# Rounding of the feed-forward weights in three VectorE operations, its range guard as a later check of refetched pieces, and the first half batch's softmax sums on TensorE

## The chip, the cores and the metric

The kernel runs on one core of one Trainium2 chip. The metric is the device time of one execution in microseconds (us). The engines are named as in the profile: PE is TensorE (PEld its weight load), DVE is VectorE, ACT is ScalarE, POOL is GpSimd and SP is SyncE, which here only issues transfers. Each engine works through its own instructions in order.

## What is computed

An attention block with routing by cluster is followed by a feed-forward block. Queries and keys attend to each other only where both have the same nearest centroid.

```python
q_assign = argmax(einsum('bhsd,hcd->bhsc', q_n, c_n), axis=-1)   # batch 4, heads 8, seq 768, dim 64
k_assign = argmax(einsum('bhsd,hcd->bhsc', k_n, c_n), axis=-1)   # 16 clusters
mask = q_assign[:, :, :, None] == k_assign[:, :, None, :]
attn = softmax(where(mask, scale * q @ k.T, -1e9))
x = (attn @ v).transpose(0, 2, 1, 3).reshape(3072, 512)
h = x @ w_in                                                     # w_in 512 x 2048
out = (h - tanh(h)) @ w_out                                      # w_out 2048 x 512
```

The two weight matrices arrive as 64-bit floats, that is as pairs of 32-bit words, and the kernel makes 32-bit floats of them on the chip.

## The kernel before

**Steps.** The work runs through 96 steps. A *block* is half of a batch's queries (8 blocks). In it four *pairs* of heads follow each other, and each pair takes three steps, of two key tiles of 128 each. In a step `begin` (L476) makes the scores of the following step: `score` (L319) multiplies on PE into a tile `sc` of the PSUM pool `ps_s`, which has two buffers, and ACT takes the exponential in place. `select` (L330) then has DVE mask them by equal cluster codes, four operations a step, into `e`; POOL adds the masked tiles up into `sum` (L346, L350). `value` (L353) multiplies `e` by `v` on PE. After a pair's third step `total` (L367) has PE sum `sum` over the partitions into `den`, ACT copies it to SBUF, POOL adds it into `wholes` (L380), and `divide` (L383) takes reciprocals on DVE, whose result POOL adds into `inverses` (L390). Both are read at the very end by a range check that decides whether a general version (`general`, L571) has to run.

**Feed-forward.** From the second block on, 28 items of `ffn_items` (L394) of the half batch before are spread over a block's 12 steps: 16 `up` items (PE multiplies by `w_in`, ACT takes tanh, DVE subtracts: `h`, `th`, `g`) and 12 `project` items (PE multiplies by `w_out` into `o`). `h`, `o` and `den` share the PSUM pool `ps_f` of three buffers. Small work (`todo`, L534) is handed out between the items of a step.

**Routing a pair.** Each later pair of heads is prepared by four stages that `ready` (L446) assigns to steps: 0 is `turn` (PE transposes of q and k into `pt`, also in `ps_s`, and two ACT copies), 1 is `similar` (PE product with the centroids into `sim`, ACT copy `simt`), 2 is `route` (PE transposes of `simt`, four DVE operations that give `code`), 3 is `publish` (a PE transpose of `code`, a DVE cast, a store to DRAM, from which `spread` loads `row` again). `sim`, the transposes of `simt` and that of `code` all lie in one buffer of `ps_s`, held from stage 1 to stage 3. Stages 1 and 2 stand at the end of one step, and stage 3 at the very start of the next, ahead of `begin`.

**Weights.** 32 pieces of 512 KB each go through three buffers `raw`, fetched by POOL's queue (L131). `round_weights` (L135) has ACT scale the low words into `rest`, DVE shift and mask the high words (L146, L150), and POOL add the two as integers (L153). `guard_weights` (L155), one piece later, has DVE take the exponent out of the high words again (L162) and multiply the result by whether it is in range (L166); only then is the `raw` buffer free and the next piece fetched. `weights_on` (L466) does one piece in each of the first block's 12 steps (two before them) and three in each step of the second block until all 32 are done, in its first six steps.

Of the kernel before, what the change touches and what calls it, by code (L numbers as in the profile page):

```python
# [28 lines left out]
F32 = mybir.dt.float32  # L29
# [7 lines left out]
P = 128  # L37
BIG = 2.0**60
F32_LEAST = 897
TINY = 1e-30  # L40
# [9 lines left out]
def kernel(  # L50
# [29 lines left out]

    const = ctx.enter_context(tc.tile_pool(name="const", bufs=1))
# [8 lines left out]
    wholes = const.tile([P, TB], F32, name="wholes")  # L90
    flag = const.tile([1, 1], I32, name="flag")
# [11 lines left out]
    ] + [(w_out[c // FQ][:, c % FQ], w_out_r[:, c]) for c in range(CF)]  # L103

    def fast():
# [27 lines left out]
        rests = {}  # L133

        def round_weights(n: int):  # L135

            if words == 1:
                return  # L140
            bits = PIECES[n][0].bitcast(U32)
            pair = raws[n].rearrange("p (n two) -> p n two", two=2)
            lo, hi = pair[:, :, 0], pair[:, :, 1]
            rest = rests[n] = outp.tile([P, FQ * P], U32, name="rest", tag="osb")
            nc.scalar.activation(out=rest, in_=lo, func=ACT.Copy, scale=2.0**-29)
            nc.vector.tensor_scalar(  # L146
                out=bits, in0=hi, scalar1=3, scalar2=0x3FFFFFF8,
                op0=ALU.logical_shift_left, op1=ALU.bitwise_and,
            )
            nc.vector.scalar_tensor_tensor(  # L150
                out=bits, in0=hi, scalar=0xC0000000, in1=bits, op0=ALU.bitwise_and, op1=ALU.bitwise_or
            )
            nc.gpsimd.tensor_tensor(out=rest, in0=bits, in1=rest, op=ALU.add)  # L153

        def guard_weights(n: int):  # L155

            if words == 1:
                return
            dst = PIECES[n][0]
            bits = dst.bitcast(U32)  # L160
            hi = raws.pop(n).rearrange("p (n two) -> p n two", two=2)[:, :, 1]
            nc.vector.tensor_scalar(  # L162
                out=bits, in0=hi, scalar1=20, scalar2=0x7FF,
                op0=ALU.logical_shift_right, op1=ALU.bitwise_and,
            )
            nc.vector.scalar_tensor_tensor(  # L166
                out=dst, in0=bits, scalar=float(F32_LEAST), in1=rests.pop(n).bitcast(F32),
                op0=ALU.is_ge, op1=ALU.mult,
            )
# [86 lines left out]
        def similar(n: int):  # L256

            ps = sims[n] = ps_s.tile([P, 2, 512], F32, name="sim", tag="s")
            for i in range(2):
                for half in range(2):  # L260
                    r = (2 * i + half) * 2 * C
                    nc.tensor.matmul(  # L262
                        ps[r : r + 2 * C, 0, 0:TB], lhsT=bd[:, pairs[n][1]],
                        rhs=turned[n, i][:, half], start=True, stop=True, tile_position=(0, r),
                    )
            t = rtp.tile([P, TB], F32, name="simt")
            nc.scalar.copy(out=t, in_=ps[:, 0, 0:TB])
            sims[n] = ps, t

        def route(n: int):  # L270

            ps, t = sims.pop(n)
            for j in range(HCH):
                nc.tensor.transpose(  # L274
                    out=ps[:, 1, j * P : (j + 1) * P], in_=t[:, j * P : (j + 1) * P], identity=ident
                )
            G = HCH * 8
            pr = ps[:, 1, 0:TB].rearrange("p (g c) -> p g c", c=C)
# [14 lines left out]
            sims[n] = ps, code  # L293

        def publish(n: int):
            ps, code = sims.pop(n)
            G = HCH * 4
            nc.tensor.transpose(  # L298
                out=ps[0:G, 0, 0:P], in_=code[:, 0].rearrange("p a h j -> p (a h j)"), identity=ident
            )  # L300
            t = rtp.tile([G, P], BF16, name="qc")
            nc.vector.tensor_copy(out=t, in_=ps[0:G, 0, 0:P])
# [27 lines left out]
        def select(n: int, half: int, j: int):  # L330
# [11 lines left out]
            if j % 2 == 1:  # L342
# [9 lines left out]
        def value(n: int, half: int, s: int):  # L352
# [11 lines left out]
        dens = {}  # L364

        def total(n: int, half: int):

# [366 lines left out]
```

## Time and profile before

| what | value |
|---|---|
| median of three runs (lowest, highest) | 1224.85 us (1223.64, 1228.05) |
| the profiled execution | 1225.34 us |
| its span, first to last instruction | 1223.6 us |
| PE busy | 1085.9 us (89%) |
| DVE busy | 550.4 us (45%) |
| POOL busy | 437.3 us (36%) |
| ACT busy | 307.3 us (25%) |

The span is what the trace shows from the first to the last instruction; 1.7 us of the profiled execution lie around it. Busy times are sums over stretches with different limits, so the table alone doesn't tell what ends last anywhere. A line of the trace's timeline has the start in us from the span's start, the duration in us (of all merged instructions), engine, source line, operation, output and inputs, the number of instructions, and in brackets the idle time of the engine before it with what ended it. A 32-bit matmul stands as two instructions in the trace.

### The profile page before, as it was taken

What the parts mean: (1) busy time and instruction counts of PE and PEld (TensorE: products, weight loads), DVE (VectorE), ACT (ScalarE), POOL (GpSimd) and SP (SyncE); (2) the same over time, 40 slices, a digit from 0 to 9 for tenths busy, and PEclk for the clock granted to TensorE, in tenths of its full rate; (3) what the DMA queues carried; (4) which work ended last, traced back from release to release, by engine and by line L of the source; (5) the groups of instructions that cost most, each with busy time, mean ns of one, the idle gap of its engine ahead of it and who ended that gap; (6) DMA issues with size and microseconds to landing.
All of it is one profiled execution on the core that took longest, in us unless ns stands there. A gap on an engine that the chain in (4) does not pass through costs nothing.

```text
span 1223.6 us, 10558 instructions
## 1 busy us (share of the span) xinstructions
PE 1085.9 (89%) x3842; PEld 506.0 (41%) x3842; DVE 550.4 (45%) x891; ACT 307.3 (25%) x491; POOL 437.3 (36%) x318
## 2 busy tenths in 40 slices
PE   3655676789889999889889999898889999999997
PEld 1222333334444445444345445443345445544543
DVE  3788998863344324333334333433334432442210
ACT  2332222222223122322123213222123223321100
POOL 1555665443223333233214432332324433443000
PEclk9777888899999999999889999999999999999999
DMA  7332234221020000112020000110000000000000
GB/s 194 104 84 71 67 118 118 83 58 54 22 52 7 9 18 13 43 44 54 22 52 7 9 9 22 33 46 32 33 20 7 16 16 9 1 9 9 9 9 21
DMA packets 66509, 49.10 MB, mean 40 GB/s; under 512 B 52624, under 2 KB 60816, under 8 KB 66448
## 3 DMA queue, kind: packets, MB, share of 16 engines
q1 hardware_dynamic: 59776, 25.22, 8.3%
q0 software_dynamic: 6528, 23.07, 5.6%
q8 instruction: 33, 0.54, 0.2%
q14 instruction: 28, 0.23, 0.1%
q10 hardware_dynamic: 144, 0.03, 0.0%
HBM read 41.98 MB, written 6.34 MB: 39 GB/s over the span
## 4 chain that ended last, share of the span: by engine, by line
PE 74%; DVE 12%; issue 9%; ACT 2%; DMA 2%; POOL 1%; SPq 0%; POOLq 0%; DVEq 0%; ACTq 0%
PE o L415 24%; PE h L402 22%; PE sc L323 13%; PE av L359 11%; DVE e L337 2%; PE den L372 2%; PE pt L244 1%; DVE w_in L150 1%; PE sim L262 1%; DVE w_in L166 1%; DVE w_out L150 1%; DMA raw<-in_moe_w_out_dram 1%; DVE den L386 1%; DVE w_in L146 1%; DVE top L287 1%
## 5 line engine op out<-in xcount | busy, mean ns | idle before, releaser
L402 PE MATMUL h<-xT,w_in 128*128 128x384 f32 x1024 | 348.4, 497 | 8.5 <-DVE g L409 8.5
L415 PE MATMUL o<-w_out,g 128*128 128x512 f32 x768 | 341.0, 598 | 0.0
L350 POOL TENSOR_TENSOR sum<-sum,e 128x768 f32<-128x768 f32 x128 | 232.1, 1813 | 275.5 <-DVE e L337 272.2
L337 DVE SCALAR_TENSOR_TENSOR e<-row,code,sc 128x384 f32<-128x384 bf16 x384 | 213.3, 608 | 258.5 <-ACT sc L328 198.8
L402 PEld LDWEIGHTS h<-xT,w_in 128*128 128x128 f32 x1024 | 193.6, 193 | 162.4 <-issue 30.2
L415 PEld LDWEIGHTS o<-w_out,g 128*128 128x128 f32 x768 | 142.4, 190 | 188.6 <-issue 184.7
L328 ACT ACTIVATE sc<-sc 128x768 f32<-128x768 f32 x192 | 146.2, 794 | 243.0 <-PE sc L323 213.7
L323 PE MATMUL sc<-t,t 64*128 64x384 f32 x768 | 180.6, 595 | 26.0 <-DVE e L337 14.4
L409 DVE TENSOR_TENSOR g<-h,th 128x384 f32<-128x384 f32 x128 | 71.1, 555 | 230.5 <-ACT th L407 230.0
L359 PE MATMUL av<-e,vals 128*64 128x384 f32 x768 | 156.3, 531 | 0.0
L407 ACT ACTIVATE th<-h 128x384 f32<-128x384 f32 x128 | 62.8, 491 | 295.3 <-PE h L402 293.1
L323 PEld LDWEIGHTS sc<-t,t 64*128 64x128 f32 x768 | 75.4, 214 | 110.2 <-issue 52.6
L380 POOL TENSOR_TENSOR wholes<-wholes,den 128x384 f32<-128x384 f32 x32 | 31.8, 993 | 198.0 <-ACT den L379 198.0
L386 DVE RECIPROCAL den<-den 128x128 f32<-128x128 f32 x96 | 83.2, 916 | 35.7 <-POOL wholes L380 35.7
L359 PEld LDWEIGHTS av<-e,vals 128*64 128x64 f32 x768 | 49.9, 146 | 103.4 <-issue 101.8
L423 POOL DMA_DIRECT2D out_dram<-osb x24 | 13.4, 558 | 165.0 <-ACT osb L422 165.0
L346 POOL TENSOR_TENSOR sum<-e 128x768 f32<-128x768 f32 x32 | 57.8, 1806 | 23.3 <-DVE e L337 22.4
L390 POOL TENSOR_TENSOR inverses<-inverses,den 128x384 f32<-128x384 f32 x32 | 43.8, 1370 | 46.4 <-DVE den L386 46.4
L298 PE MATMUL sim<-ident,code 128*12 128x128 f32 x16 | 5.4, 340 | 53.1 <-DVE code L289 53.1
L422 ACT COPY osb<-o 128x512 f32<-128x512 f32 x24 | 14.1, 589 | 145.7 <-PE o L415 145.7
L244 PE MATMUL pt<-ident,x 128*128 128x128 f32 x192 | 29.0, 306 | 22.7 <-DMA x<-in_q_dram 8.4
L282 DVE TENSOR_REDUCE mx<-sim 128x24 f32<-128x384 f32 x16 | 8.9, 555 | 73.9 <-PE sim L274 73.9
(66 smaller groups left out, 434.9 us busy)
## 6 DMA issues: line engine op xcount, KB each, us to landing
raw<-in_moe_w_in_dram POOLq DMA_DIRECT2D x16, 512.0 KB, 4.1
raw<-in_moe_w_out_dram POOLq DMA_DIRECT2D x16, 512.0 KB, 3.8
x<-in_q_dram SPq DMA_DIRECT2D x32, 192.0 KB, 3.8
x<-in_k_dram SPq DMA_DIRECT2D x32, 192.0 KB, 4.6
vals<-in_v_dram SPq DMA_DIRECT2D x32, 192.0 KB, 2.5
row<-q_codes SPq DMA_DIRECT2D x32, 192.0 KB, 3.2
out_dram<-osb POOLq DMA_DIRECT2D x24, 256.0 KB, 2.3
q_codes<-qc SPq DMA_DIRECT2D x16, 3.0 KB
```

Of the source, the lines that this page charges most:

```text
L323: nc.tensor.matmul(sc[:, h, 0:TB], lhsT=turned[n, 1][r].rearrange("p a n -> p (a n)")[:, j * P : (j + 1) * P], rhs=turned[n, 0][r, half], ...
L328: nc.scalar.activation(out=sc[:, :, 0:TB], in_=sc[:, :, 0:TB], func=ACT.Exp, scale=SCALE)
L337: nc.vector.scalar_tensor_tensor(out=e[:, h], in0=rows[n, half][:, h], scalar=codes[n][:, 1, j // HCH, h, j % HCH : j % HCH + 1], in1=sc[: ...
L346: nc.gpsimd.tensor_tensor(out=s, in0=pair[:, 0], in1=pair[:, 1], op=ALU.add)
L350: nc.gpsimd.tensor_tensor(out=s, in0=s, in1=pair[:, i], op=ALU.add)
L359: nc.tensor.matmul(avs[n, half][h * D : h * D + D], lhsT=vals[n][:, h, j], rhs=e[:, i, h], start=(j == 0), stop=(j == NCH - 1),)
L386: nc.vector.reciprocal(out=t[:, c], in_=t[:, c])
L390: nc.gpsimd.tensor_tensor(out=inverses, in0=inverses, in1=dens.pop((n, half)), op=ALU.add)
L402: nc.tensor.matmul(h, lhsT=w_in[i][:, c, o * P : (o + 1) * P], rhs=xT[b, half][:, c], start=(c == 0), stop=(c == CD - 1),)
L407: nc.scalar.activation(out=th, in_=h, func=ACT.Tanh)
L409: nc.vector.tensor_tensor(out=gs[i][:, o], in0=h, in1=th, op=ALU.subtract)
L415: nc.tensor.matmul(acc[sub], lhsT=gs[i][:, o, sub * P : (sub + 1) * P], rhs=w_out[i][:, o], start=(i == 0 and o == 0), stop=(i == NQ4 - 1 ...
```

## The change

- `assemble` replaces both `round_weights` and `guard_weights`: ACT scales the low words into `rest` as before, DVE shifts and masks (two operations), and DVE adds `rest` instead of POOL. The guard's two DVE operations per piece and POOL's add go away. The piece's `raw` buffer is free right after, and the next fetch follows at once.
- `check_weights`: when all 32 pieces are rounded, every piece is fetched again, one a step, and one DVE operation takes the smallest magnitude of its high words into a column of `smallest`. That joins the range check at the end (two small DVE operations more). `general` rounds and guards the pieces itself, in a branch that these inputs don't take.
- In the first block (`early`) the sums of `e` are made on PE: four matmuls a step with `ones` accumulate in `den`, in a buffer of `ps_f` that a pair holds for its three steps. POOL's sums and the summing matmuls of `total` go away there.
- `sim`, the transposes of `simt` (`pr`) and of `code` (`pq`) get buffers of `ps_f` of their own, each freed after its read, instead of one of `ps_s`.
- Stage 1 moves to the start of the next step, ahead of `begin`; stage 0 comes right after `select`; stages 2 and 3 come last in their steps, 3 one step after 2. Before the first step, `select` comes ahead of the second pair's preparation.

```diff
+    def assemble(dst, raw, rest):
+        nc.scalar.activation(out=rest, in_=lo, func=ACT.Copy, scale=2.0**-29)
+        nc.vector.tensor_scalar(
+            out=bits, in0=hi, scalar1=3, scalar2=0x3FFFFFF8,
+            op0=ALU.logical_shift_left, op1=ALU.bitwise_and,
+        )
+        nc.vector.scalar_tensor_tensor(
+            out=bits, in0=hi, scalar=0xC0000000, in1=bits, op0=ALU.bitwise_and, op1=ALU.bitwise_or
+        )
+        nc.vector.tensor_tensor(out=bits, in0=bits, in1=rest, op=ALU.add)
...
+        def check_weights(n: int):
             hi = raws.pop(n).rearrange("p (n two) -> p n two", two=2)[:, :, 1]
+            nc.vector.tensor_reduce(
+                out=smallest[:, n : n + 1], in_=hi.bitcast(F32), axis=AX.X, op=ALU.min,
+                apply_absolute_value=True,
             )
...
-            ps = sims[n] = ps_s.tile([P, 2, 512], F32, name="sim", tag="s")
+            ps = ps_f.tile([P, TB], F32, name="sim", tag="f")
...
+            ps = ps_f.tile([P, TB], F32, name="pr", tag="f")
...
+            ps = ps_f.tile([G, P], F32, name="pq", tag="f")
...
+            if early(n, half):
+                if s == 0:
+                    sums[n, half] = ps_f.tile([P, TB], F32, name="den", tag="f")
+                for i in range(2):
+                    for h in range(2):
+                        nc.tensor.matmul(
+                            sums[n, half][h * D : h * D + D], lhsT=ones, rhs=e[:, i, h],
+                            start=(s + i == 0), stop=(2 * s + i == NCH - 1),
+                        )
...
         def weights_on():
+            nonlocal done
+            if done < len(PIECES):
+                round_weights(done)
+            elif done < 2 * len(PIECES) and words == 2:
+                check_weights(done - len(PIECES))
+            done += 1
+            fetch()
...
-            if 3 in stages:
-                stages.pop(3)()
+            if 1 in stages:
+                stages[1]()
...
+            if 0 in stages:
+                todo.append(stages[0])
             todo += late
...
-            todo += [stages[i] for i in sorted(stages)]
+            todo += [weights_on] * (3 if block == 1 and done < len(PIECES) else 1)
+            todo += [stages[i] for i in (2, 3) if i in stages]
```

What this does to the order of instructions is shown at two places. The first is DVE in the first block, from a pair's third piece of weights to the division of its sums; `e` is the masked tile, `den` the sums. Before:

```order
L146 TENSOR_SCALAR w_in_69<-raw 128x512
L150 SCALAR_TENSOR_TENSOR w_in_69<-raw,w_in_69 128x512
L162 TENSOR_SCALAR w_in_69<-raw 128x512
L166 SCALAR_TENSOR_TENSOR w_in_69<-w_in_69,rest 128x512
L337 SCALAR_TENSOR_TENSOR e<-row,code,sc 128x384 x4
L386 RECIPROCAL den<-den 128x128 x3
L389 TENSOR_TENSOR xT<-xT,den 128x384
```

And with the change, the same place on DVE:

```order
L118 TENSOR_SCALAR w_in_69<-raw 128x512
L122 SCALAR_TENSOR_TENSOR w_in_69<-raw,w_in_69 128x512
L125 ISA w_in_69<-w_in_69,rest 128x1024
L335 SCALAR_TENSOR_TENSOR e<-row,code,sc 128x384 x4
L399 RECIPROCAL den<-den 128x128 x3
L402 TENSOR_TENSOR xT<-xT,den 128x384
```

The guard's two operations have gone, and the integer add has come from POOL; it is built as one special instruction on 1024 halves of words instead of 512 words.

The second place is PE where a later pair is routed, at the end of a block's projections; `simt` and `code` are what the transposes read, `sim` and `pr` what they write. Before:

```order
L415 MATMUL o<-w_out_73,g 128x512 x4
L262 MATMUL sim<-t_2662,bd 32x384 x2
L262 MATMUL sim<-t_2671,bd 32x384 x2
L274 MATMUL sim<-ident,simt 128x128 x3
L298 MATMUL sim<-ident,code 12x128
L323 MATMUL sc<-t_2349,t_2358 128x384 x4
L359 MATMUL av<-e,vals 64x384 x4
L372 MATMUL den<-sum,ones 64x384 x2
L415 MATMUL o<-w_out_74,g 128x512 x4
L415 MATMUL o<-w_out_75,g 128x512 x4
```

And with the change, the same pair on PE:

```order
L243 MATMUL pt<-ident,x_2401 128x128 x6
L261 MATMUL sim<-t_2722,bd 32x384 x2
L261 MATMUL sim<-t_2731,bd 32x384 x2
L321 MATMUL sc<-t_1663,t_1672 128x384 x4
L357 MATMUL av<-e,vals 64x384 x4
L428 MATMUL o<-w_out_73,g 128x512 x4
L428 MATMUL o<-w_out_74,g 128x512 x4
L274 MATMUL pr<-ident,simt 128x128 x3
L321 MATMUL sc<-t_2387,t_2396 128x384 x4
L357 MATMUL av<-e,vals 64x384 x4
L385 MATMUL den<-sum,ones 64x384 x2
L428 MATMUL o<-w_out_75,g 128x512 x4
```

`sim`, the transposes of `simt` and that of `code` stood back to back on PE, ahead of the next scores. Now scores, values and projections stand between `sim` and `pr`, the transpose of `code` (`pq`) comes two rows behind the last one shown, and `sim` follows right on the transposes `pt` of its stage 0.

## Rows read from the trace of the kernel before

**Rows 1.** Stretches: length; busy us (count) by engine; PE's clock, DMA share, GB/s.

```profile
42.00:141.00 99.00, 59.63 (x248) 24.73 (x248) 90.86 (x110) 31.95 (x48) 61.60 (x47) 0.74 0.28 79
141.00:254.00 113.00, 85.96 (x292) 41.49 (x288) 101.04 (x138) 34.11 (x58) 61.18 (x54) 0.86 0.32 100
327.00:1124.00 797.00, 767.10 (x2764) 357.56 (x2764) 298.85 (x516) 202.49 (x326) 278.15 (x182) 0.98 0.08 23
```

**Rows 2.** DVE's groups, 42 to 141 us: busy us, mean ns | idle before, releaser.

```profile
L337 DVE SCALAR_TENSOR_TENSOR e<-row,code,sc 128x384 f32<-128x384 bf16 x44 | 24.2, 604 | 7.0 <-ACT sc L328 6.6
L150 DVE SCALAR_TENSOR_TENSOR w_in<-raw,w_in 128x512 uint32<-128x512 uint32 x11 | 19.5, 1774 | 0.4
L166 DVE SCALAR_TENSOR_TENSOR w_in<-w_in,rest 128x512 f32<-128x512 uint32 x11 | 18.0, 1634 | 0.4
L146 DVE TENSOR_SCALAR w_in<-raw 128x512 uint32<-128x512 uint32 x11 | 13.2, 1198 | 0.0
L386 DVE RECIPROCAL den<-den 128x128 f32<-128x128 f32 x9 | 7.7, 912 | 1.2 <-POOL wholes L380 1.2
L162 DVE TENSOR_SCALAR w_in<-raw 128x512 uint32<-128x512 uint32 x11 | 4.6, 416 | 0.0
```

**Rows 3.** Timeline of one step of the first block, from 42 us.

```profile
42.35 2.83 PE L359 MATMUL av<-e,vals 128*64 128x384 f32 x8
43.36 3.77 POOL L350 TENSOR_TENSOR sum<-sum,e 128x768 f32<-128x768 f32 x2 [3.02 <-DVE e L337]
45.50 2.18 DVE L150 SCALAR_TENSOR_TENSOR w_in<-raw,w_in 128x512 uint32<-128x512 uint32 x1
...
48.05 1.63 DVE L166 SCALAR_TENSOR_TENSOR w_in<-w_in,rest 128x512 f32<-128x512 uint32 x1
```

**Rows 4.** DVE's timeline: each pair's first select, and one L150 between.

```profile
57.12 2.18 DVE L337 SCALAR_TENSOR_TENSOR e<-row,code,sc 128x384 f32<-128x384 bf16 x4
...
63.94 0.69 DVE L150 SCALAR_TENSOR_TENSOR w_in<-raw,w_in 128x512 uint32<-128x512 uint32 x1
...
86.88 2.18 DVE L337 SCALAR_TENSOR_TENSOR e<-row,code,sc 128x384 f32<-128x384 bf16 x4
...
117.27 2.18 DVE L337 SCALAR_TENSOR_TENSOR e<-row,code,sc 128x384 f32<-128x384 bf16 x4
...
141.34 2.18 DVE L337 SCALAR_TENSOR_TENSOR e<-row,code,sc 128x384 f32<-128x384 bf16 x4
```

**Rows 5.** DVE's groups, 141 to 254 us, same columns as rows 2.

```profile
L409 DVE TENSOR_TENSOR g<-h,th 128x384 f32<-128x384 f32 x16 | 8.7, 547 | 0.5 <-ACT th L407 0.5
L146 DVE TENSOR_SCALAR w_out<-raw 128x512 uint32<-128x512 uint32 x16 | 8.7, 544 | 3.6 <-DMA raw<-in_moe_w_out_dram 3.6
```

**Rows 6.** PE's waits, 254 to 1130 us: us in total, times, longest.

```profile
PE sim L298 <- DVE code L289: 27.4, 11, 2.5
PE sim L274 <- ACT simt L267: 6.6, 11, 0.6
```

**Rows 7.** Timeline of PE and ACT at one routed pair, near 500 us.

```profile
498.83 1.47 PE L244 MATMUL pt<-ident,x 128*128 128x128 f32 x12
499.68 1.50 ACT L250 COPY t<-pt 128x768 f32<-128x768 f32 x2 [0.16 <-PE pt L244]
500.53 1.62 PE L323 MATMUL sc<-t,t 64*128 64x384 f32 x8 [0.23 <-ACT t L250]
...
513.37 0.38 PE L298 MATMUL sim<-ident,code 128*12 128x128 f32 x1 [2.49 <-DVE code L289]
513.68 2.87 PE L323 MATMUL sc<-t,t 64*128 64x384 f32 x8
...
523.92 1.56 PE L323 MATMUL sc<-t,t 64*128 64x384 f32 x8
```

**Rows 8.** Of the page: one group of POOL, one of transfers.

```profile
L380 POOL TENSOR_TENSOR wholes<-wholes,den 128x384 f32<-128x384 f32 x32 | 31.8, 993 | 198.0 <-ACT den L379 198.0
...
raw<-in_moe_w_out_dram POOLq DMA_DIRECT2D x16, 512.0 KB, 3.8
```

More of the change, by code (lines that the diff above doesn't have):

```diff
@@ L39 @@
 F32_LEAST = 897
+HIGH_LEAST = 2.0**-15 * 1.125
 TINY = 1e-30
@@ L79 @@
     assert H * C == P and 2 * D == P and H * D == DM and CD == HP
+    len_pieces = NQ4 * CD + CF
     const = ctx.enter_context(tc.tile_pool(name="const", bufs=1))
@@ L90 @@
     wholes = const.tile([P, TB], F32, name="wholes")
+    smallest = const.tile([P, len_pieces], F32, name="smallest")
     flag = const.tile([1, 1], I32, name="flag")
@@ L140, in round_weights @@
                 return
[L141 to L160, printed above, removed]
-            hi = raws.pop(n).rearrange("p (n two) -> p n two", two=2)[:, :, 1]
[L162 to L168, printed above, removed]
+            rest = outp.tile([P, FQ * P], U32, name="rest", tag="osb")
+            assemble(PIECES[n][0], raws.pop(n), rest)
+        def check_weights(n: int):
+            hi = raws.pop(n).rearrange("p (n two) -> p n two", two=2)[:, :, 1]
+            nc.vector.tensor_reduce(
+                out=smallest[:, n : n + 1], in_=hi.bitcast(F32), axis=AX.X, op=ALU.min,
+                apply_absolute_value=True,
             )
@@ L341, in select @@
                 )
-            if j % 2 == 1:
+            if j % 2 == 1 and not early(n, half):
                 pair = weights[n, half, j // 2]
@@ L362, in value, with early @@
                     )
+            if early(n, half):
[7 more added lines that the diff above has]
+                        )
         dens = {}
+        def early(n: int, half: int):
+            return n < HP and half == 0
         def total(n: int, half: int):
@@ L369, in total @@
             s = sums.pop((n, half))
-            ps = ps_f.tile([P, TB], F32, name="den", tag="f")
-            for h in range(2):
-                nc.tensor.matmul(
-                    ps[h * D : h * D + D], lhsT=ones, rhs=s[:, h], start=True, stop=True
-                )
+            ps = s
+            if not early(n, half):
+                ps = ps_f.tile([P, TB], F32, name="den", tag="f")
+                for h in range(2):
+                    nc.tensor.matmul(
+                        ps[h * D : h * D + D], lhsT=ones, rhs=s[:, h], start=True, stop=True
+                    )
             if p == 0:
@@ L500, in fast @@
         begin(steps[0])
+        weights_on()
+        for i in range(2):
+            select(*steps[0][:2], i)
         turn(1, 1, nc.scalar)
@@ L503, in fast @@
         similar(1)
-        weights_on()
-        for i in range(2):
-            select(*steps[0][:2], i)
         route(1)
@@ L576, in general @@
         nc.vector.tensor_copy(out=identb, in_=ident)
+        for dst, src in PIECES if words == 2 else ():
+            raw = gs.tile([P, 2 * FQ * P], U32, name="graw")
+            nc.sync.dma_start(raw, src)
+            rest = gs.tile([P, FQ * P], U32, name="grest")
+            assemble(dst, raw, rest)
+            nc.vector.tensor_scalar(
+                out=rest, in0=raw.rearrange("p (n two) -> p n two", two=2)[:, :, 1], scalar1=20,
+                scalar2=0x7FF, op0=ALU.logical_shift_right, op1=ALU.bitwise_and,
+            )
+            nc.vector.scalar_tensor_tensor(
+                out=dst, in0=rest, scalar=float(F32_LEAST), in1=dst, op0=ALU.is_ge, op1=ALU.mult
+            )
         cnT = gs.tile([D, H, C], F32, name="cnT")
```

49 lines of the change are left out of this document (22 added, 27 removed).

## Prediction

> **What bounds the kernel now.** I read the stretches first, then DVE's groups in the early ones, the timeline of one step, and last PE's waits in the rest. Three regimes show [rows 1]. From 42 to 141 us (the first block) DVE is busy 90.9 of 99 us, PE 59.6, and PE's granted clock is 0.74, between its levels of 1.2 and 2.4 GHz (0.5 and 1). From 141 to 254 us (the second block up to its last rounded piece) DVE is busy 101 of 113 us, PE 86. From 327 us on PE is busy 96% of the time and DVE 37%. So DVE work counts ahead of 254 us, and PE's work and idle time behind it.
>
> The early DVE time is mostly not work. In the first block one weight piece costs the sum of L146, L150, L162 and L166: (13.2 + 19.5 + 4.6 + 18.0) / 11 = 5.0 us [rows 2]. L150 takes 0.69 us when POOL has nothing to add, and 2.18 us when it has [rows 4, 3]: the one at 45.50 starts beneath two POOL adds that run from 43.36 to 47.13, and ends 0.55 us behind them. So these operations of DVE, which read and write SBUF alone, stand still while POOL adds. L166 carries about 0.95 us of the same behind POOL's integer add, and L146 about 0.8. Alone the four would take 0.41 + 0.69 + 0.41 + 0.69 = 2.2 us.
>
> Late, PE waits 27.4 us for `code` and 6.6 us for `simt`, at 11 routed pairs [rows 6]: `sim`, its transposes and that of `code` stand in a row on PE, with ACT's copy and four DVE operations in between. After the 2.49 us wait the eight score matmuls take 2.87 us; elsewhere 1.56 [rows 7]. That is PE at its lower level after the gap.
>
> **Term A, the first block.** DVE loses two operations a piece and gains the add. No row has that add on DVE. The nearest is L150 alone, 0.69 us on as many bytes. The change builds it on 1024 halves of words; at L150's time for 512 elements that is twice 0.69, 1.38 us, the upper bound. I take 0.69, by bytes. The Trainium skill (VectorE: DVE Perf Modes, "The perf-mode tier table") has `tensor_tensor` take two 16-bit elements a cycle with both inputs in SBUF, and one 32-bit element. By that page the add would take what 512 words take, 691 ns by its formula, and the sum would stay as it is; no trace here shows it.
>
> A piece then takes 0.41 + 0.69 + 0.69 = 1.8 us instead of 5.0, for POOL's adds of `e` and its integer adds are gone from this block. That is 35 us off DVE for 11 pieces, but not off the time: PE and the chain come next. I follow a pair from `select` to `select`:
> - A step without extras: DVE 2.2 + 1.8 = 4.0; PE scores 1.56, values 1.5 (2.83 at the lower level, [rows 3]), and the new sums, as many matmuls as the values, 1.5: 4.6 us. PE ends last.
> - The step after `turn`: 1.47 for the transposes, whose buffers `select` has to free, two copies of 0.75 [rows 7], then `sim`, scores, exponential and `select`: 8.3 us.
> - The step with the division: the values and sums end 0.9 us after `select`; two ACT copies and POOL's 0.99 [rows 8] make it 2.8 until DVE can start three reciprocals, 2.6 [rows 2]; product 0.6, a wait of 0.8 for POOL's add into `inverses`, piece 1.8, the four routing operations 2.2, `select` 2.2: 12.9 us, and 10.6 without routing.
>
> Routing and turning fall into different pairs: what is left of the first pair 4.5 + 8.3 = 12.8 us; the second 12.9 + 4.3 + 8.3 = 25.5 (29.8 now, [rows 4]); the third, with routing alone, 12.9 + 4.5 + 4.5 = 21.9 (30.4); the fourth 10.6 + 9.4 = 20.0 (24.1). That is 80.2 for 99.3 us, less 0.7 because the second piece's copy now stands behind the first exponentials on ACT, ahead of the first `select`: 18 us. The 4.6 us of a plain step hold PE at its upper level, which 0.74 does not promise; I take 3 us back. **Gain 15 us.** Bounds: 30 if DVE still ended every step, and -6 if PE ran at the lower level throughout (scores 2.9, values 2.8, sums 2.8 = 8.6 us in each of some six plain steps).
>
> **Term B, 141 to 254 us.** Here POOL's sums stay (3.8 us in a step, [rows 3]); its integer adds and the guard go. A step on DVE: `select` 2.2, three pieces 5.4, two or three `g` of 0.55 [rows 5], and 2.8 of standing behind POOL's sums: 11.5 to 12. A division adds 3.1 but meets less POOL work; the routing adds 2.2. Seven intervals: 9 + 12 + 12 + 13.5 + 12 + 13.5 + 13.5 = 85.5 us. PE's work in this stretch is at most its 86 us, some of it at the lower level, so PE is next, close behind. I take 90 for the 113. **Gain 23 us.** Bounds: 30 (83 us) and 13 (100 us, where the two engines' waits add).
>
> **Term C, the routed pairs.** 27.4 + 6.6 + 11 x 1.3 (scores at the lower level) = 48 us on PE. In the new order the transposes of `simt` come a step's projections after `sim`, and that of `code` a further step's matmuls after `route`; both waits go. What is late next is `sim`, right behind `pt`: it needs both copies, 0.75 each after transposes of 0.75 each, some 0.9 us where the scores now wait 0.23 [rows 7]: 0.7 x 11 = 7.7 us. **Gain 41 us.** Bounds: 48, and 25 if `sim` waits 2.1 us each time.
>
> **At nothing.** The checks: 32 DVE operations of 512 elements, 0.69 us each by L150, 22 us on a DVE that is busy 37% while PE ends last; without that cover 22 us more. The second fetches: 32 transfers of 512 KB that land in 3.8 us [rows 8], at a DMA share of 0.08 [rows 1]; POOL's queue is held at each fetch until DVE has checked, and behind it stand the next step's sums, which can start only after a later `select` anyway. The two closing DVE operations lie under the last projections. Stage 3 a step's work later: `row` is first loaded in the step after it and used two steps on, behind about 10 us of work for a store and a load.
>
> **Sum.** 1223.6 - 15 - 23 - 41 = 1144.6 us of span, and 1.7 us around it: 1146 us. The profiled execution's 1225.34 stands 0.5 us from the median, so the figure holds for the median too.
>
> **Rivals.**
> - *The add is one half word at a time.* 0.69 us more for 14 pieces of the first block, of which some 8 lie on the chain, and for 18 of the second: 5.5 + 12.4 = 18 us: 1164 us. For it: the instruction covers 1024 elements. Against: the bytes are L150's. 0.15. The same page of the Trainium skill gives one element a cycle to what misses its conditions, such as a step of one.
> - *PE stays at its lower level in the first block*, since gaps remain at every division: term A is -6, 1167 us. For it: 0.74 today, and 2.8 us values [rows 3]. Against: the sums on PE fill gaps. 0.13.
> - *The routing gap only moves.* `sim`, `pr`, `pq`, `h`, `o` and `den` now share three buffers, and a wait for a buffer takes the place of that for `code`: term C is 0, 1187 us. Against: each buffer's reader comes at least a scores-and-values pair, 3 us, ahead of the next use. 0.12.
> - *Slower: POOL's queue.* If each of the 26 checks after 254 us made PE wait for a landing (3.8 us) since sums stand behind the fetch, 26 x 3.8 = 99 us would be lost: 1245 us. It turns slower from 3.0 us a check on. `raw` waits exist today, 3.6 us in all [rows 5]. Against: POOL has 65% of that stretch free, three buffers run ahead, and PE needs the sums once in three steps. 0.04.
>
> **How the numbers follow.** The forecast has 0.54, and alone would span 1129 (bounds 18 + 30 + 48 = 96, without the far end of A) to 1164. To hold 8 in 10 the range takes in the first two rivals and the low bounds of A and C together, and leaves out the last two: 1120 to 1185 us. 0.5% is about 6 us, which is what a measurement of this kernel can tell from no change. All cases but the last lie over 30 us below today; a mix of bad ends near zero gets 0.02: faster 0.94, same 0.02, slower 0.04.
>
> **What would show it.** Right: pieces in the first block of 1.8 us with L122 at 0.69; L125 at 0.69; pairs of 20 to 26 us there; the second block's rounding over near 216 us; no PE wait for `code` late, scores at 1.56 behind routing, a wait of about 0.9 us before `sim`. Wrong: L125 at 1.4; PE waiting for DVE in plain steps of the first block; waits of PE at `h`, `o` or `den` for a buffer; POOL idle at a fetch with `den` late behind it.

## The result, and the profile after

The changed kernel takes 1125.45 us (median of four runs, 1124.45 to 1126.44), beside 1224.96 us for the kernel before: a ratio of 0.9184, 95% interval 0.9165 to 0.9204, so 8.2% faster. The profiled execution has a span of 1124.5 us at a mean granted clock of 0.987; before it was 1223.6 us at 0.943. The forecast was 1146 us. The time lies in its range, but 20 us below the forecast and 4 us below the span of 1129 to 1164 that the forecast gave itself. The gain is 99.1 us of span where 79 were forecast, and each of the three terms was taken too small.

The three stretches that answer to [rows 1], with the same columns (length; busy us and count of PE, PEld, DVE, ACT, POOL; PE's clock, DMA share, GB/s). The first two are cut at the same selects as before, and the third ends as far ahead of the program's end; it is 100 us shorter, so only its shares compare.

```profile
43.00:122.00 79.00, 62.34 (x318) 25.48 (x316) 58.94 (x99) 30.36 (x46) 12.87 (x17) 0.88 0.35 100
122.00:204.00 82.00, 75.93 (x297) 37.57 (x297) 75.95 (x117) 34.34 (x60) 38.95 (x36) 0.98 0.46 138
327.00:1024.00 697.00, 695.14 (x2538) 324.69 (x2538) 287.31 (x491) 183.52 (x295) 267.76 (x188) 1.00 0.13 37
```

In the first block neither PE (79%) nor DVE (75%) is near full any more; the two wait for each other. In the second block DVE is still busy 93% of the time and ends the steps. Late, PE is busy 99.7% at the full clock (96% and 0.98 before).

**First block.** DVE's timeline, `select` only (start, duration, and in brackets the idle time before it with what ended it). The pairs start at 43.47, 56.00, 81.38 and 104.92, and the second block at 122.21, answering to [rows 4].

```profile
43.47 1.14 DVE L335 SCALAR_TENSOR_TENSOR e<-row,code,sc 128x384 f32<-128x384 bf16 x2 [2.19 <-ACT sc L326]
...
56.00 2.19 DVE L335 SCALAR_TENSOR_TENSOR e<-row,code,sc 128x384 f32<-128x384 bf16 x4 [1.36 <-ACT sc L326]
68.12 2.18 DVE L335 SCALAR_TENSOR_TENSOR e<-row,code,sc 128x384 f32<-128x384 bf16 x4
72.31 2.17 DVE L335 SCALAR_TENSOR_TENSOR e<-row,code,sc 128x384 f32<-128x384 bf16 x4
81.38 2.19 DVE L335 SCALAR_TENSOR_TENSOR e<-row,code,sc 128x384 f32<-128x384 bf16 x4 [1.37 <-ACT sc L326]
...
104.92 2.19 DVE L335 SCALAR_TENSOR_TENSOR e<-row,code,sc 128x384 f32<-128x384 bf16 x4 [3.12 <-DMA row<-q_codes]
...
122.21 2.19 DVE L335 SCALAR_TENSOR_TENSOR e<-row,code,sc 128x384 f32<-128x384 bf16 x4 [1.31 <-ACT sc L326]
```

The second pair shows the three kinds of step: with division and routing 12.1 us (56.00 to 68.12), plain 4.2, after `turn` 9.1. In the plain step DVE goes from select to select without a pause. What the 12.1 us consist of shows the timeline of all engines in that step:

```profile
59.07 1.00 POOL L393 TENSOR_TENSOR wholes<-wholes,den 128x384 f32<-128x384 f32 x1 [4.34 <-ACT den L392]
...
60.10 2.58 DVE L399 RECIPROCAL den<-den 128x128 f32<-128x128 f32 x3 [1.91 <-POOL wholes L393]
...
63.19 1.22 DVE L118 TENSOR_SCALAR w_in<-raw 128x512 uint32<-128x512 uint32 x1
...
65.27 0.69 DVE L125 CUSTOM_DVE_ANT_0 w_in<-w_in,rest 128x1024 uint16<-128x1024 uint16 x1
...
67.65 0.55 DVE L287 TENSOR_REDUCE code<-top 128x24 f32<-128x384 f32 x1
...
68.35 0.37 PE L296 MATMUL pq<-ident,code 128*12 128x128 f32 x1 [5.20 <-DVE code L287]
...
69.39 2.93 PE L321 MATMUL sc<-t,t 64*128 64x384 f32 x8 [0.67 <-DVE e L335]
```

DVE stands 1.91 us waiting for POOL's `wholes`, then does the reciprocals, the piece and the four routing operations in that order; PE waits 5.20 us for `code` meanwhile. The scores behind that wait take 2.93 us, at a granted clock of 0.50 (68.3 to 72.3 us), and wait 0.67 us for DVE. The add that came to DVE (L125) takes 0.69 us, as taken in the prediction.

**Second block.** Timeline of DVE and POOL in one step:

```profile
133.86 3.78 POOL L348 TENSOR_TENSOR sum<-sum,e 128x768 f32<-128x768 f32 x2 [1.27 <-DVE e L335]
...
135.14 0.82 DVE L118 TENSOR_SCALAR w_in<-raw 128x512 uint32<-128x512 uint32 x1
136.00 2.19 DVE L122 SCALAR_TENSOR_TENSOR w_in<-raw,w_in 128x512 uint32<-128x512 uint32 x1
138.33 0.69 DVE L125 CUSTOM_DVE_ANT_0 w_in<-w_in,rest 128x1024 uint16<-128x1024 uint16 x1
...
139.41 0.42 DVE L118 TENSOR_SCALAR w_in<-raw 128x512 uint32<-128x512 uint32 x1
139.86 0.69 DVE L122 SCALAR_TENSOR_TENSOR w_in<-raw,w_in 128x512 uint32<-128x512 uint32 x1
```

Beneath POOL's sums the first piece's shift takes 0.82 and its mask 2.19 us, standing still 0.4 + 1.5 = 1.9 us; the next pieces take 0.42 and 0.69. That answers to [rows 3].

**Late.** PE's waits over the whole span (us in total, times, longest):

```profile
PE pq L296 <- DVE code L287: 15.3, 4, 5.2
...
PE sc L321 <- DVE e L335: 5.5, 4, 3.2
...
PE h L415 <- DVE top L282: 4.0, 1, 4.0
PE sim L261 <- ACT t L249: 3.0, 13, 0.2
PE h L415 <- DVE g L422: 1.8, 2, 1.4
```

The 27.4 and 6.6 us of [rows 6] are gone: the four waits for `code` that are left lie ahead of 204 us, and behind it there are only 11 of the 13 for the copy `t`. The waits of `sc` for DVE's `e` lie in the first block. Of the waits for a buffer that the third rival names there are three, at `h` in the second block: 4.0 us until `route` has read its `pr`, and 1.8 us in two for `g`. A routed pair on PE, near 460 us, answers to [rows 7]:

```profile
456.52 0.27 PE L296 MATMUL pq<-ident,code 128*12 128x128 f32 x1
...
466.63 1.47 PE L243 MATMUL pt<-ident,x 128*128 128x128 f32 x12
468.33 1.54 PE L261 MATMUL sim<-t,bd 128*32 128x384 f32 x8 [0.23 <-ACT t L249]
469.81 1.56 PE L321 MATMUL sc<-t,t 64*128 64x384 f32 x8
...
490.68 0.27 PE L296 MATMUL pq<-ident,code 128*12 128x128 f32 x1
```

And the checks among DVE's groups from 204 us on (busy us, mean ns, idle before):

```profile
L165 DVE TENSOR_REDUCE smallest<-raw 128x1 f32<-128x512 f32 x32 | 21.6, 676 | 0.0
```

### The profile page after: what moved, and what is told of

It reads as the page before. It is cut to its first block, busy times and chain, and to the rows that moved or that the text cites. A ratio compares the mean times of both kernels' runs of the same rounds, so it can differ in the third digit from the quotient of the medians.

```text
span 1124.5 us, 10709 instructions
## 1 busy us (share of the span) xinstructions
PE 1063.1 (95%) x3922; PEld 500.6 (45%) x3922; DVE 509.9 (45%) x893; ACT 304.7 (27%) x491; POOL 377.9 (34%) x298
## 3 DMA queue, kind: packets, MB, share of 16 engines
q0 software_dynamic: 11136, 39.85, 11.1%
## 4 chain that ended last, share of the span: by engine, by line
PE 78%; issue 9%; DVE 9%; DMA 1%; ACT 1%; POOL 1%; SPq 0%; POOLq 0%; DVEq 0%; ACTq 0%
PE o L428 26%; PE h L415 23%; PE sc L321 12%; PE av L357 11%; PE sim L261 2%; DVE e L335 2%; PE den L385 1%; DVE w_out L122 1%; PE pt L243 1%; DVE den L399 1%; ACT t L249 1%; PE den L366 1%; DMA x<-in_k_dram 1%; DVE w_out L125 1%; DVE w_out L118 1%
## 5 line engine op out<-in xcount | busy, mean ns | idle before, releaser
L415 PE MATMUL h<-xT,w_in 128*128 128x384 f32 x1024 | 344.0, 492 | 5.8 <-DVE top L282 4.0
L348 POOL TENSOR_TENSOR sum<-sum,e 128x768 f32<-128x768 f32 x112 | 202.5, 1808 | 260.1 <-DVE e L335 257.4
L321 PE MATMUL sc<-t,t 64*128 64x384 f32 x768 | 155.8, 524 | 5.8 <-DVE e L335 5.5
L357 PE MATMUL av<-e,vals 128*64 128x384 f32 x768 | 148.5, 508 | 0.0
L321 PEld LDWEIGHTS sc<-t,t 64*128 64x128 f32 x768 | 68.1, 191 | 83.8 <-issue 56.6
L357 PEld LDWEIGHTS av<-e,vals 128*64 128x64 f32 x768 | 47.4, 138 | 89.9 <-issue 87.2
L344 POOL TENSOR_TENSOR sum<-e 128x768 f32<-128x768 f32 x28 | 50.4, 1802 | 5.1 <-DVE e L335 5.1
L153 POOL DMA_DIRECT2D raw<-in_moe_w_in_dram x32 | 18.3, 571 | 88.7 <-DVE w_in L122 60.1
L249 ACT COPY t<-pt 128x768 f32<-128x768 f32 x31 | 23.5, 801 | 69.9 <-PE pt L243 69.9
```

Source lines behind the costliest of these rows:

```text
L321: nc.tensor.matmul(sc[:, h, 0:TB], lhsT=turned[n, 1][r].rearrange("p a n -> p (a n)")[:, j * P : (j + 1) * P], rhs=turned[n, 0][r, half], ...
L344: nc.gpsimd.tensor_tensor(out=s, in0=pair[:, 0], in1=pair[:, 1], op=ALU.add)
L348: nc.gpsimd.tensor_tensor(out=s, in0=s, in1=pair[:, i], op=ALU.add)
L357: nc.tensor.matmul(avs[n, half][h * D : h * D + D], lhsT=vals[n][:, h, j], rhs=e[:, i, h], start=(j == 0), stop=(j == NCH - 1),)
L415: nc.tensor.matmul(h, lhsT=w_in[i][:, c, o * P : (o + 1) * P], rhs=xT[b, half][:, c], start=(c == 0), stop=(c == CD - 1),)
```

## The experiments

Each is the changed kernel with the edit shown. A ratio is to the kernel before on the same chip, with its 95% interval; the changed kernel's is 0.9184 (0.9165 to 0.9204). Lengths of blocks and steps are read from each run's profiled execution, from `select` to `select`.

### Which part of the change brings how much

**Order and pools alone.** The old rounding, guard, add on POOL and single fetch are put back, and POOL makes the sums everywhere; `e5b_order_sums` keeps the first block's sums on PE (without the last edit).

```diff
-            assemble(PIECES[n][0], raws.pop(n), rest)
...
+            nc.gpsimd.tensor_tensor(out=rest, in0=bits, in1=rest, op=ALU.add)
...
+            if guarded < done - 1 or guarded == len(PIECES) - 1:
+                guard_weights(guarded)
...
-            return n < HP and half == 0
+            return False
```

> The changed kernel's order and pools of the routing stages, with the rounding, guard and single fetch of the kernel before and its sums on POOL in the first block. Theory 'round trips': the late gain of 49 us stays whole, and the early rounding costs what it did, less the waits for code in the first two blocks: 1160 to 1172 us. Rival 'the parts need each other' (the new order gains only where DVE has time): late 49 us lost to slower first blocks, 1180 to 1195 us.

Measured: 1164.26 us, 0.9504 (0.9488 to 0.952), as expected. The order and the pools alone bring 60.7 of the 99.5 us. Of the two profiles' difference 48.9 us lie behind the second block's rounding and 12.5 ahead of its end, where the second block takes 103.6 us instead of 112.8 and the first 95.8 instead of 99.3.

> As the order alone, but with the first block's sums on PE. Theory 'standing still': with the old rounding each of the first block's pieces is rid of the wait behind POOL's two sums (0.8 at L146 and 1.5 at L150), in all steps, since DVE ends every step there: 15 to 25 us below the order alone, 1138 to 1155 us. Rival: as with the new rounding, the sums on PE come out even: within 5 us of the order alone.

Measured: 1154.75 us, 0.9422 (0.9407 to 0.9438), 9.5 us below the run without the sums on PE. By what it saves that is between the two theories' figures (15 to 25 us, and up to 5), though the time is still within the first one's range by a hair; it bears out neither. The block's first selects show why: the first block gets 11.5 us shorter (95.8 to 84.4 us), and the second 2 us longer.

From 1154.75 to 1125.45 us, 29 us, is the new rounding. Its largest part is the guard:

**The guard beside the rounding on DVE**, five operations a piece, no second fetch.

```diff
             assemble(PIECES[n][0], raw, rest)
+            nc.vector.tensor_scalar(
+                out=rest, in0=raw.rearrange("p (n two) -> p n two", two=2)[:, :, 1], scalar1=20,
+                scalar2=0x7FF, op0=ALU.logical_shift_right, op1=ALU.bitwise_and,
+            )
+            nc.vector.scalar_tensor_tensor(
+                out=PIECES[n][0], in0=rest, scalar=float(F32_LEAST), in1=PIECES[n][0],
+                op0=ALU.is_ge, op1=ALU.mult,
+            )
```

> The changed kernel with the guard back beside the rounding, on DVE, so five DVE operations a piece and none on POOL; the second fetches and checks are left out. Theory 'own time': the guard's two operations cost 1.1 us on DVE for each of 18 pieces in the second block, 20 us, and 0.5 to 1.1 us in most steps of the first, 8 to 10 us: 1148 to 1157 us. Rival 'only its waits cost' (what the guard cost was standing behind POOL's integer add and holding the raw buffer): 1128 to 1137 us.

Measured: 1150.5 us, 0.9389 (0.9375 to 0.9404): 25 us slower than the changed kernel, as the theory of its own time has it. The guard costs its own two operations, 0.43 + 0.69 us, in steps that DVE ends: a step of three pieces in the second block takes 14.6 us instead of 11.1.

**Without the later check.** The weights' range guard is left out, with its second fetch.

```diff
-                check_weights(done - len(PIECES))
+                return
...
-            if fetched < (1 if words == 1 else 2) * len(PIECES):
+            if fetched < len(PIECES):
```

> The changed kernel without the second fetches and without the checks (the range guard of the weights is left out altogether). Theory 'covered': 32 operations of 0.68 us on DVE and 32 transfers lie under PE: within 4 us of the changed kernel, 1121 to 1127 us. Rival 'POOL's queue is held at the fetches, and sums and division come late behind it': each of 32 costs up to 0.7 us, 1103 to 1115 us.

Measured: 1123.35 us, 0.9165 (0.915 to 0.918). The interval overlaps that of the changed kernel, so the 2.1 us are not more than the runs can tell. The traces are sharper: at all twelve later pairs, from the first behind 190 us to the last behind 800, `pq` comes 0.91 or 0.92 us later here than in the changed kernel, and so does the last store. So 21.6 us of checks and 32 transfers of 512 KB are wholly covered there, and what the two times differ by lies outside. The guard's gain is real: the same test costs 25 us early and nothing late.

In a row the runs give the whole way: 1224.96 us, 1164.26 with the order and the pools, 1154.75 with the first block's sums on PE, 1150.5 with the add on DVE and the guard beside it, 1123.35 without a guard, 1125.45 with the later check.

**The add on POOL again**, all else as changed.

```diff
-        nc.vector.tensor_tensor(out=bits, in0=bits, in1=rest, op=ALU.add)
+        nc.gpsimd.tensor_tensor(out=bits, in0=bits, in1=rest, op=ALU.add)
```

> The changed kernel, but POOL and not DVE adds rest to the shifted words, straight into the weight tile; the guard stays a later check. Theory 'standing still': in the first block POOL's 1.3 us lie under select, which reads PSUM and doesn't wait, and PE ends the plain steps anyway; in the second block the next piece's L118 and L122 wait behind that add and lose what DVE saves: 1121 to 1132 us. Rival 'number of operations': 0.69 us less on DVE for each of 18 pieces in the second block, where DVE is busy all the time: 1110 to 1114 us.

Measured: 1120.66 us, 0.9146 (0.9131 to 0.9162), 4.8 us *faster* than the changed kernel. That is just below the range of the one theory and far from the other's; the two intervals stand just clear of each other. Moving the add to DVE was a loss by itself. The timeline of this kernel shows the add on POOL:

```profile
51.58 0.69 ACT L117 ACTIVATE rest<-raw 128x512 uint32<-128x512 uint32 x1
...
52.36 1.26 POOL L125 TENSOR_TENSOR w_in<-w_in,rest 128x512 uint32<-128x512 uint32 x1 [5.63 <-ACT rest L117]
...
54.36 2.19 DVE L335 SCALAR_TENSOR_TENSOR e<-row,code,sc 128x384 f32<-128x384 bf16 x4 [4.21 <-ACT sc L326]
```

The add waits for ACT's `rest`, which stands behind other work on ACT. In the changed kernel that wait stops DVE's queue; of the 7.2 us ahead of the 11 adds of the first block it makes 5.9 (DVE's group from 43 to 122 us; the columns are those of [rows 2]):

```profile
L125 DVE CUSTOM_DVE_ANT_0 w_in<-w_in,rest 128x1024 uint16<-128x1024 uint16 x11 | 7.6, 692 | 7.2 <-ACT rest L117 5.9
```

It looks like the cause, but the steps speak against it. The 5.9 us are two waits, of 2.15 and 3.78 us, and the `select` behind each waits 1.36 or 1.37 us more, for ACT's exponential (56.00 and 81.38 above). With the add on POOL the first of these selects waits 4.21 us for the same exponential, and its step takes 7.46 us for 7.45. The second's step is 0.8 us shorter, with PE's values ahead of it at 1.72 us instead of 2.83. What gets shorter are steps that DVE ends: the two with division and routing by 0.65 us each (11.46 and 11.52 for 12.12 and 12.17), and the plain step behind each by 0.35 (3.84 for 4.19). The other steps of the block change by up to 2 us each way, and by 0.25 us in sum; the block takes 76.5 us instead of 78.7.

The second block takes 79.2 us instead of 82.3, but not by the add's own time. DVE's adds, 13.2 us there, fall away, and its shifts and masks take 44.0 us instead of 31.2, since they stand still beneath POOL's integer adds too. What is saved is the idle time ahead of DVE's adds, 3.0 us. Ahead of the first block the two profiles differ by 2.1 us more, as executions of these kernels do: the select at 43.47 stands between 41.3 and 44.2 us in them.

### POOL's sums and DVE

**The first block's sums on POOL** (`early` returns False).

> The changed kernel, but the first block's sums of e stay on POOL as they were (no tile takes its sums on PE while it is being made). Theory 'standing still' (DVE's operations on SBUF alone wait while POOL adds): in the first block L118 goes from 0.42 to about 0.8 and L122 from 0.69 to about 2.2 us in steps with two adds, as they do in the second block of the changed kernel, so six plain steps get 1.7 us longer and the division steps about 0.5: 1135 to 1140 us, although PE has 15 us less to do. Rival 'number of operations' (what was gained is two operations of DVE per piece and POOL's adds don't matter): PE is rid of 1.5 us in each plain step that PE ends, 1114 to 1120 us.

Measured: 1127.96 us, 0.9203 (0.9188 to 0.9219), 2.5 us above the changed kernel, which is neither theory's figure; the intervals overlap. By stretches it is clear nevertheless: the first block is 5.3 us longer (84.0 for 78.7 us), and the second 2.5 us shorter. In the second block the first step takes 7.9 us instead of 10.4, and DVE starts its reciprocals there at once, where the changed kernel has it wait 2.04 us for `wholes`.

**POOL makes the first block's sums too, and nobody reads them**; PE's stay.

```diff
-            if j % 2 == 1 and not early(n, half):
+            if j % 2 == 1:
...
+                    s = spare[n, half] = sump.tile([P, 2, TB], F32, name="sum")
+                    if not early(n, half):
+                        sums[n, half] = s
```

> The changed kernel, whose first block's sums are made on PE, with POOL making the same sums as well, into tiles that nobody reads: POOL's old adds with nothing else changed. Theory 'standing still': DVE loses 1.9 to 2.3 us in each of some six plain steps and about 0.5 in the others: 1134 to 1142 us. Rival 'POOL's adds don't matter to DVE': 1124 to 1127 us.

Measured: 1129.4 us, 0.9218 (0.9203 to 0.9233): 4 us, less than the one theory and more than the other. The cause is there, as one plain step shows (the one that takes 4.2 us from 68.12 in the changed kernel, and 6.5 here):

```profile
69.23 3.75 POOL L350 TENSOR_TENSOR sum<-sum,e 128x768 f32<-128x768 f32 x2 [3.15 <-DVE e L335]
70.04 1.28 DVE L118 TENSOR_SCALAR w_in<-raw 128x512 uint32<-128x512 uint32 x1
71.36 2.17 DVE L122 SCALAR_TENSOR_TENSOR w_in<-raw,w_in 128x512 uint32<-128x512 uint32 x1
73.67 0.69 DVE L125 CUSTOM_DVE_ANT_0 w_in<-w_in,rest 128x1024 uint16<-128x1024 uint16 x1
```

The shift takes 1.28 instead of 0.42 and the mask 2.17 instead of 0.69 us, though nothing depends on POOL's result. The Trainium skill (SBUF — State Buffer, "Who interferes with whom") has VectorE and GpSimd share one pair of SBUF ports, and calls it an exclusive lock; this trace agrees, with 2.17 for 0.69 us. But where DVE waits for scores, a slower piece delays nothing: the first block grows by 6.0 us (84.8 for 78.7), not by 2.3 us for each of its 11 pieces, and 2.5 come back in the second block.

### The routed pairs

**The stages where they stood before**, in the new buffers.

```diff
-            if 1 in stages:
-                stages[1]()
+            if 3 in stages:
+                stages.pop(3)()
...
-            todo += [stages[i] for i in (2, 3) if i in stages]
+            todo += [stages[i] for i in sorted(stages)]
```

> The changed kernel with the four routing stages in their old places (similar and route together at the end of a step, publish at the start of the next, ahead of the scores); their tiles stay in the pool ps_f. Theory 'round trips': PE waits again 2.5 us for code and 0.6 for simt at each of 11 late pairs, and the scores behind take 2.9 instead of 1.56: 48 us there, and some 10 to 15 us in the first two blocks: 1175 to 1190 us. Rival 'buffers' (the late gain came from giving the scores both buffers of ps_s back): within 6 us of the changed kernel, 1119 to 1132 us.

Measured: 1184.72 us, 0.9663 (0.9647 to 0.9679), 59 us slower, as the theory of the round trips has it, with PE's wait back:

```profile
PE pq L296 <- DVE code L287: 53.2, 16, 7.9
```

Late, a period of two blocks (four routed pairs, from `pq` to `pq`) takes 276.4 us. It was 278.3 before and is 259.3 with the change, so of the 19 us that a period gained the new buffers alone bring 1.9 (and 0.25 in the next period, 277.75 for 278.0).

**The new places, the tiles in `ps_s`** (`sim` shown; `pr` and `pq` likewise).

```diff
-            ps = ps_f.tile([P, TB], F32, name="sim", tag="f")
+            ps = ps_s.tile([P, 2, 512], F32, name="sim", tag="s")[:, 0, 0:TB]
```

> The changed kernel with the three routing tiles in the scores' pool of two buffers again, each a short-lived tile of its own, in the new order. Theory 'round trips': most of the gain stays, but the second score tile waits for DVE to have read the transposes of simt, 1 to 2.5 us at 11 late pairs and 3 to 5 in two early ones: 1140 to 1160 us. Rival 'the pool doesn't matter': 1122 to 1130 us.

Measured: 1150.3 us, 0.9389 (0.9374 to 0.9405), 25 us slower, again as the theory of the round trips has it. PE now waits for a buffer that DVE has to free:

```profile
PE sc L321 <- DVE top L282: 26.5, 14, 7.5
```

A late period takes 263.5 us here: the order saves 15 of the 19 us and the pool the rest. Of this pool's 25 us, 15 lie ahead of the `pq` at which this period starts (317.4 for 302.3 us). So late it is the order that ends the round trips, and the pool adds the last 4 us. Every run with the new order gives each of the three tiles a buffer of its own; what one buffer, held through all stages, would cost with it is not shown.

### Two edits in search of more

**The division one step later**, behind the next `select` (a block's last pair excepted).

```diff
-            todo += late
-            late = []
+            todo += due
+            due = late if p < HP - 1 else []
+            todo += late if p == HP - 1 else []
+            late = []
```

> The changed kernel with a pair's division (three reciprocals and the product) a step later, behind the next step's select, except for a block's last pair. Theory 'the division's wait': DVE waits some 2 us for POOL's add in three pairs of the first block, and PE 5.2 us for code behind it; both shrink, 5 to 9 us: 1116 to 1121 us. Rival 'only moved': the division's 3.1 us delay the select behind them as much: 1122 to 1128 us.

Measured: 1114.36 us, 0.9092 (0.9077 to 0.9108), 11.1 us faster than the changed kernel, more than expected. In the step that had PE wait 5.20 us, routing now comes ahead of the reciprocals (all engines, names as above):

```profile
62.29 0.55 DVE L287 TENSOR_REDUCE code<-top 128x24 f32<-128x384 f32 x1
62.76 2.18 DVE L335 SCALAR_TENSOR_TENSOR e<-row,code,sc 128x384 f32<-128x384 bf16 x4
63.03 0.28 PE L296 MATMUL pq<-ident,code 128*12 128x128 f32 x1
...
64.86 2.57 DVE L399 RECIPROCAL den<-den 128x128 f32<-128x128 f32 x3
```

`pq` waits for nothing, and the first block is 5.3 us shorter. Some 6 us more were not in the theory, and lie after 257 us. The division now stands behind `turn` in the list of small work that is spread over a step's projections. The list is longer, so `turn` falls one item of four projection matmuls earlier (x8 in the trace). PE near 457 us:

```profile
457.07 1.47 PE L243 MATMUL pt<-ident,x 128*128 128x128 f32 x12
458.38 3.60 PE L428 MATMUL o<-w_out,g 128*128 128x512 f32 x8
461.91 0.85 PE L261 MATMUL sim<-t,bd 128*32 128x384 f32 x8
```

`sim` takes 0.85 us here, and 1.54 with a wait of 0.23 ahead of it in the changed kernel: it stood 0.92 us for the two copies of ACT, most of it hidden in the duration of the group. From `pq` to `pq` the pair takes 33.17 instead of 34.16 us, at three of four pairs.

**Both: the add on POOL and the late division**, and the same with the first block's sums on POOL.

> The changed kernel with two of the single edits together: the add of rest on POOL, and a pair's division a step later. If both gains add (11 and 5 us): 1108 to 1111 us. If one covers the other: 1112 to 1116 us.

Measured: 1105.79 us (1105.03 to 1106.88), 0.9025 (0.9013 to 0.9037). This is the fastest version, 9.75% under the kernel before. The two gains of 4.8 and 11.1 us add, and 3.8 us more come on top, which was not expected: the first block takes 66.6 us, where each edit alone gives 76.5 and 73.4 for 78.7. Most of it is in the fourth pair: with the add on POOL alone its division waits 1.98 us for `wholes`, and the pair gets 2.0 us longer (19.3 for 17.3); with the late division this wait is gone, and the add's leaving makes the pair 1.5 us shorter (14.4 for 15.9).

> As the kernel with the add on POOL and the later division, with the first block's sums on POOL too. Theory 'standing still': POOL's adds now hold DVE in every step of that block, and the division no longer waits behind PE's sums, so what made both places of the sums even is gone: 4 to 12 us slower than that kernel, 1113 to 1122 us. Rival 'even': within 3 us of it.

Measured: 1109.88 us, 0.9055 (0.9041 to 0.9069): 4.1 us slower than that version, at the low end of the difference that was expected (the time itself is below the range, since that version came out faster than was counted on); the sums on PE are worth 4 us there.

## Why the prediction was right, and where it was too small

**The mechanisms held.** DVE's standing still behind POOL, the guard's cost, the round trip at the routed pairs and the cover of the checks are each shown by a run (`e11_extra_sums`, `e8_guard_dve`, `e3_old_stages`, `e4_no_check`). The sizes of all three terms were too cautious, and which engine ends the first block's plain steps was wrong.

**Term A: 15 us forecast, 19.1 measured** (141.34 to 122.21 for the block's end). The walk from select to select gave 12.8, 25.5, 21.9 and 20.0 us for the pairs; measured are 12.5, 25.4, 23.5 and 17.3, a sum of 78.7 for 80.2. Within that, the third pair has a wait of 3.1 us for `row` that no step named, and the fourth wins 2.7 back behind it: its division starts without a wait, and that step takes 7.9 us instead of 10.6. So the sum's closeness is in part luck. The plain step is 0.4 us shorter, and not ended by PE as walked: DVE goes through it without a pause, and PE waits 0.67 us for `e`, one of the signs of being wrong that the prediction named. The second pair's step after `turn` is 0.8 longer. The start shifts by 1.4 instead of 0.7 us, which is within what executions differ by. What failed most is the deduction of 3 us for PE's lower level. PE does fall to it behind each wait for `code` (0.50 from 68.3 to 72.3 us, scores 2.93 and values 2.83 us), but DVE ends the plain step there, and only the 0.8 us of the step behind it show; over the block the clock rose from 0.74 to 0.88.

**Term B: 23 us forecast, 30.4 measured** (82.3 for 112.8 us), at its bound of 30. DVE's sum of 85.5 us was the right way to cost it, and the 4.5 us on top, for PE being close behind, were not needed: DVE, busy 93%, ends the steps. The term names only the rounding, though. By the runs 9.1 of the 30.4 us are the new order's (`e5_order_alone`), the first block's sums on PE take 2.1 back, and the rounding brings 23.4 (from 105.7 us in `e5b_order_sums`). Standing behind POOL's sums is 1.9 us a step, not 2.8, since only one piece of three meets them.

**Term C: 41 us forecast, 49.5 measured**, above its bound of 48. PE's groups over one late period of four routed pairs tell why, first of before (352.08 to 630.38 us), then of after (302.30 to 561.60 us); columns as in [rows 2]:

```profile
L323 PE MATMUL sc<-t,t 64*128 64x384 f32 x192 | 42.7, 569 | 0.9 <-ACT t L250 0.9
L359 PE MATMUL av<-e,vals 128*64 128x384 f32 x192 | 38.5, 524 | 0.0
...
L262 PE MATMUL sim<-t,bd 128*32 128x384 f32 x32 | 3.4, 498 | 0.0
...
L298 PE MATMUL sim<-ident,code 128*12 128x128 f32 x4 | 1.3, 326 | 10.0 <-DVE code L289 10.0
```

```profile
L321 PE MATMUL sc<-t,t 64*128 64x384 f32 x192 | 37.5, 508 | 0.0
L357 PE MATMUL av<-e,vals 128*64 128x384 f32 x192 | 36.3, 499 | 0.0
...
L261 PE MATMUL sim<-t,bd 128*32 128x384 f32 x32 | 6.2, 498 | 0.9 <-ACT t L249 0.9
```

For each pair, the wait for `code` gives back 2.5 us, that for `simt` 0.6, and the scores 1.3, all as forecast. `sim` costs 0.7 us more, again as forecast: the new wait of 0.9 us is there, but a reader of the waits alone sees 0.2 of it, since the rest lies within the 1.54 us of the group. What the sum left out is the values behind those scores, which ran at the lower level too: 0.55 us a pair, and 0.15 for the other small groups. At one pair of before:

```profile
589.01 2.93 PE L323 MATMUL sc<-t,t 64*128 64x384 f32 x8
591.87 2.83 PE L359 MATMUL av<-e,vals 128*64 128x384 f32 x8
```

In all this is 4.4 us a pair, or 48 for 11, where the forecast had 3.7. The period shows 19.0 / 4 = 4.75; 0.35 us a pair stays unassigned.

**At nothing: held.** The checks take 21.6 us for the forecast 22, and leaving them out changes nothing that can be told. POOL's queue behind the fetches held nobody up: leaving them out shortens no stretch between two `pq` by more than 0.02 us, which rules out the slower rival.

**The rivals.** The add half word by half word would have shown 1.4 us; L125 shows 0.69. PE at its lower level in the first block: that holds only behind each wait for `code` or `e`; the granted clock rose to 0.88 over the block. The gap that only moves: with the tiles in `ps_f` one wait of 4.0 us for their buffers is left. `e7_routing_ps_s` makes a like case in the other pool; it costs 25 us, not the whole term.

**What the prediction did not ask** is whether every part of the change helps. It counted the add on DVE at 0.69 us a piece, had PE end the first block's plain steps, so that the add was free there, and took the end of POOL's integer adds as part of the gain. The run with the add on POOL shows that moving the add cost 5 us; the early gain came from the guard, the order and the sums.

## What to carry to other kernels

When an operation moves to an engine that ends the steps, its own time and the idle time ahead of it count in full, and both have to be set against what it holds up where it was. A long wait ahead of an instruction proves nothing by itself: look at what the next instruction of that engine waits for, and compare the step with a run in which the first one is elsewhere. A test that needs no answer before the end belongs in the stretch where its engine is idle, even if its data have to be fetched twice. After a round trip is taken off PE's queue, count the work behind the gap at the lower clock level too, and look for a wait inside a group by comparing its duration with the same group elsewhere.

## What the runs showed of the hardware

- The integer add of 512 words, built as one instruction over 1024 half words, took DVE 0.692 us (mean of 11), as long as a mask of 512 words alone (0.69), and POOL 1.26 us. The Trainium skill (VectorE: DVE Perf Modes, "The perf-mode tier table") caps a `tensor_tensor` on two SBUF inputs at one 32-bit element or two 16-bit elements a cycle. By either, an estimate from the same page's formula for a `tensor_tensor` add is 691 ns; the trace agrees.
- DVE's shift and mask, which touch SBUF alone, stood still beneath POOL's adds (the mask 2.17 us instead of 0.69), whether or not anyone needed POOL's result. `select`, which reads PSUM, did not: 0.6 us an operation with and without.
- On PE, the lower clock level behind a wait of 2.49 us reached past the eight score matmuls into the values. At the pair shown above the granted clock was 0.50 from 588.7 to 594.6 us; PE had been busy 0.6 us of the 3.7 before. Over a period of 24 steps the values took 38.5 us before, and 36.3 (1.51 us a step) without the wait.
